# Dilated attention turned in strands of two heads and two classes, with turns issued ahead of outputs

## The chip, the core and the metric

The program runs on one core of one Trainium2 chip. TensorE (PE) multiplies, VectorE (DVE) and ScalarE (ACT) copy its results out of PSUM and do the pointwise work, GpSimd (POOL) does pointwise work on SBUF, and SyncE (SP) issues nearly all DMAs. The metric is device microseconds for one execution.

## What is computed

Attention over 4 batch entries and 8 heads of 576 positions and 64 features, all in fp32, then a mixture of 8 experts over the 2304 tokens, then a second feed-forward layer. Heads 0 to 3 look at the last 32 positions (plain), heads 4 to 7 at every fourth of the last 128 (dilated):

```python
scores = scale * np.matmul(q, k.transpose(0, 1, 3, 2))
mask_plain = (rel >= 0) & (rel < window)                                    # window = 32
mask_dil = (rel >= 0) & (rel < window * dilation) & (rel % dilation == 0)   # dilation = 4
attn = np.exp(scores - scores.max(-1)); attn = attn / attn.sum(-1)          # masked scores: -1e9
attn_out = np.matmul(attn, v)
...
out += P[:, e:e + 1] * (np.maximum(x @ w1[e], 0.0) @ w2[e])                 # 8 experts, P by 8 normalizations
out = g(out @ w_in) @ w_out
```

## The kernel before

The attention runs in eight stages n = 0 to 7: stage n is batch entry n // 2, plain heads where n is even, dilated heads where it is odd. In a dilated stage a position is 4 i + r; positions of one class r (0 to 3) only see each other, so that 576 positions fall into four runs of 144 in which the dilated window is a plain window of 32. The kernel reads queries, keys and values in that order (`classes`, L634) and treats both kinds alike afterwards.

Each stage has three blocks g of 192 positions and each block two groups h, one for each half of TensorE's rows: 48 groups in all, and a group is one step of the schedule. Work on one group:

- `load_qk` (L698) brings queries and keys into `at.big` in six pieces of 96 positions, 256 bytes in a row; one home serves stages 0 and 2 to 7, and another stage 1. `load_v` (L709) brings values.
- `turn_qk` (L726) transposes a third of the queries or keys of a stage (tile pt, four transposes of 96 columns), and VectorE copies pt to qt or kt (L740, L744). `turn_plan` (L840) says at which step which third is turned.
- `Group.both` (L757) makes the scores s of an even group and the odd one after it with 12 matmuls; in stages 0 and 1 the mask is added by TensorE, later by VectorE (L782). `scores` takes the maximum, `exps` (L786) three exponentials with their sums on ScalarE, `norm` (L793) divides on POOL.
- `Group.turn` (L799) transposes e (tile pe, three transposes) and copies it to et, by VectorE for odd groups (L806) and by ScalarE for even ones (L808).
- `Group.out` (L810) multiplies et of both groups by the values (tile px, 12 matmuls, of 64 columns each), and both engines copy px to xf (L831, L833).

`attention_steps` (L861) issues the step i as: scores of group i, norm of i - 2, query and key turns, exps of i - 1, then, at odd i, the output of i - 4, then the turn of i - 3. It yields four times a step. From the end of stage 1 on the caller weaves in the first expert's products (ph, py) and the gate (pg) at every fourth yield; `share` says how many. `first_weights` (L1017) loads that expert's weights in quarters, the first matrix of which is split into high and low parts at steps 9 to 12, and `plain_x` does the same with the first block of its input. After the attention all remaining matmuls follow, 128 x 128 products without a break.

The order on every engine is the order of the program. PSUM has eight banks; pe, px and, from stage 3 on, pt share two of them (tag "t"), and a tile waits until its bank's last tile has been copied out. SP's queue issues DMAs one after another, and each waits until the one eight before it has landed.

Of the kernel before, what the change touches and what calls it, by code (L numbers as in the profile page):

```python
# [27 lines left out]
def tile_attention_moe_ffn(ctx: ExitStack, tc, q, k, v, w_gate, w1, w2, w_in, w_out, out):  # L28
# [605 lines left out]
    def classes(d, a, n):  # L634
# [58 lines left out]
    def raw_of(n, which):  # L693
        t0 = 0 if n == 1 else 6
        return (at.big[:CH, t0 + 3 * which:t0 + 3 * which + 3, :].rearrange("p a e -> p (a e)")
                .rearrange("p (c h x) -> p c h x", c=S // CH, h=HQ))

    def load_qk(n, which, t, second=None):  # L698

        b, d = kinds[n]  # L700
        raw = raw_of(n, which)
        src = (q, k)[which][b, d * HQ:(d + 1) * HQ]
        for c in (2 * t, 2 * t + 1):
            for off, r, i, m in classes(d, c * CH, CH):
                x = (src.rearrange("h (i r) e -> r i h e", r=DILATION)[r, i:i + m] if d
                     else src[:, i:i + m].rearrange("h i e -> i h e"))
                (second if second and c % 2 else nc.sync).dma_start(out=raw[off:off + m, c], in_=x)

    def load_v(n, g, pool):  # L709
# [4 lines left out]
        else:  # L714
            t = pool.tile([KW, JG, HQ, D], F32, tag="v", bufs=4, name=f"v{n}_{g}")
        src = v[b, d * HQ:(d + 1) * HQ]
        for j in range(JG):
            for off, r, i, m in classes(d, key0(g * JG + j), KW):
                x = (src.rearrange("h (i r) e -> r i h e", r=DILATION)[r, i:i + m] if d
                     else src[:, i:i + m].rearrange("h i e -> i h e"))  # L720
                nc.sync.dma_start(out=t[off:off + m, j], in_=x)
# [4 lines left out]
    def turn_qk(n, which, t, tag):  # L726


        raw = raw_of(n, which)
        third = S // 3  # L730
        pt = bank(tag, at.bufs[tag], f"pt{n}_{which}_{t}")[:, :NPAIR * third].rearrange(
            "p (a x) -> p a x", a=NPAIR)
        for pr in range(NPAIR):
            for i in range(2):
                nc.tensor.transpose(pt[:, pr, i * CH:(i + 1) * CH],
                                    raw[:, 2 * t + i, 2 * pr:2 * pr + 2, :].rearrange("p h e -> p (h e)"),
                                    ident[:CH, :CH])
        to = (at.qt, at.kt)[which][n % 2][:, :, t * third:(t + 1) * third]
# [4 lines left out]
        else:  # L743
            nc.vector.tensor_scalar(out=to, in0=pt, scalar1=SCALE, scalar2=None, op0=ALU.mult)  # L744

    class Group:
# [52 lines left out]
        def turn(self):  # L799
# [3 lines left out]
            self.et = self.pool.tile([KW, JG, P], F32, tag="et", bufs=2, name="et")  # L803
# [6 lines left out]
        def out(self, vt):  # L810
# [9 lines left out]
            for pr in range(NPAIR):  # L820
                c = d * NPAIR + pr
                for off, r, i, m in classes(d, g * JG * QB, JG * QB):
                    while m:

                        n0 = b * S + (DILATION * i + r if d else i)
                        step = DILATION if d else 1
                        k, x = divmod(n0, PASS)
                        w = min(m, -(-(PASS - x) // step))
                        dst = xf[:, k, c, x:x + (w - 1) * step + 1:step]
                        if pr:  # L830
                            nc.vector.tensor_copy(out=dst, in_=px[:, pr, off:off + w])  # L831
                        else:
                            nc.scalar.activation(out=dst, in_=px[:, pr, off:off + w], func=AF.Copy)  # L833
# [585 lines left out]
```

## Time and profile before

| | |
|---|---|
| median of 3 runs | 1970.97 us (1967.09 to 1972.43) |
| profiled execution | 1966.19 us, span 1964.4 us |
| PE busy | 1933.1 us (98%), 13223 matmuls |
| VectorE, ScalarE, POOL busy | 1484.5, 994.5, 313.8 us |
| mean granted TensorE clock | 0.993 |
| DMA | 539.45 MB, mean 275 GB/s |
| chain that ended last | PE 92%, DVE 4%, ACT 2%, DMA 1% |

PE is the bottleneck by its busy share, but a share over the whole span mixes the attention, about a tenth of it, with the long rest. The page's 40 slices, of 49 us each, keep them apart. In rows of the order of time the number in brackets is the time an engine stood idle before the row, and behind it is what ended that. A matmul in fp32 leaves two records, a transpose one. The end of a matmul is modelled, so idle times of PE are somewhat short.

### The profile page before, as it was taken

What the parts mean: (1) busy time and instruction counts of PE and PEld (TensorE: products, weight loads), DVE (VectorE), ACT (ScalarE), POOL (GpSimd) and SP (SyncE); (2) the same over time, 40 slices, a digit from 0 to 9 for tenths busy, and PEclk for the clock granted to TensorE, in tenths of its full rate; (3) what the DMA queues carried; (4) which work ended last, traced back from release to release, by engine and by line L of the source; (5) the groups of instructions that cost most, each with busy time, mean ns of one, the idle gap of its engine ahead of it and who ended that gap; (6) DMA issues with size and microseconds to landing.
All of it is one profiled execution on the core that took longest, in us unless ns stands there. A gap on an engine that the chain in (4) does not pass through costs nothing.

```text
span 1964.4 us, 34940 instructions
## 1 busy us (share of the span) xinstructions
PE 1933.1 (98%) x13223; PEld 1839.7 (94%) x13223; DVE 1484.5 (76%) x2632; ACT 994.5 (51%) x2131; POOL 313.8 (16%) x327
## 2 busy tenths in 40 slices
PE   7899999999999999999999999999999999999999
PEld 5777889899898989999999999999999999999999
DVE  6755698888888868686888668678886576876867
ACT  4545545454555445544445435434454455675555
POOL 4213133434535400001001000010010000000000
PEclk8899999999999999999999999999999999999999
DMA  7532577788788888899889977988898877787874
GB/s 176 117 74 82 204 269 279 300 315 306 295 321 306 335 335 307 304 324 331 288 317 332 317 264 285 343 295 317 294 334 308 285 253 279 263 290 267 290 242 144
DMA packets 222392, 539.45 MB, mean 275 GB/s; under 512 B 81040, under 2 KB 113296, under 8 KB 199824
## 3 DMA queue, kind: packets, MB, share of 16 engines
q1 hardware_dynamic: 220624, 536.82, 77.6%
q8 instruction: 105, 1.72, 0.4%
q10 hardware_dynamic: 1600, 0.39, 0.1%
q14 instruction: 63, 0.52, 0.1%
HBM read 383.53 MB, written 153.62 MB: 273 GB/s over the span
## 4 chain that ended last, share of the span: by engine, by line
PE 92%; DVE 4%; ACT 2%; DMA 1%; issue 0%; SPq 0%; ACTq 0%; DVEq 0%
PE pa L414 22%; PE py L414 16%; PE pc L414 11%; PE qy L414 9%; PE qh L414 9%; PE qt L414 9%; PE pb L414 5%; PE qs L414 3%; PE ph L414 3%; PE qx L414 1%; PE px L818 1%; PE s L769 1%; PE pe L802 1%; DMA w_kept<-raw 1%; DVE et L806 1%
## 5 line engine op out<-in xcount | busy, mean ns | idle before, releaser
L414 PE MATMUL pa<-xo,w1o 128*128 128x384 f32 x2736 | 512.9, 335 | 4.0 <-ACT kept L429 2.9
L414 PEld LDWEIGHTS pa<-xo,w1o 128*128 128x128 f32 x2736 | 476.3, 188 | 8.0 <-ACT kept L429 4.5
L414 PE MATMUL pc<-xo,w1o 128*128 128x384 f32 x1368 | 257.1, 335 | 0.8 <-DVE w1o L112 0.8
L138 POOL TENSOR_TENSOR raw<-raw 128x256 f32<-128x256 f32 x152 | 140.3, 952 | 701.5 <-DVE raw L326 170.4
L414 PE MATMUL py<-w2o,hh 128*128 128x512 f32 x816 | 251.5, 389 | 0.0
L414 PEld LDWEIGHTS pc<-xo,w1o 128*128 128x128 f32 x1368 | 238.5, 188 | 1.1 <-DVE w1o L112 1.1
L429 ACT ACTIVATE kept<-pa 128x384 f32<-128x384 f32 x228 | 110.2, 491 | 233.4 <-PE pa L414 231.7
L414 PEld LDWEIGHTS py<-w2o,hh 128*128 128x128 f32 x816 | 152.8, 188 | 30.3
L387 DVE TENSOR_TENSOR xf<-xf 128x768 f32<-128x768 f32 x180 | 167.3, 964 | 1.4
L414 PE MATMUL py<-w2o,hl 128*128 128x512 f32 x408 | 158.7, 389 | 0.0
L112 DVE TENSOR_TENSOR w1o<-raw,w1o 128x256 fp32r<-128x256 f32 x210 | 130.3, 671 | 9.8 <-ACT w1o L111 9.8
L111 ACT ACTIVATE third<-xf 128x768 fp32r<-128x768 f32 (+1 forms) x124 | 95.3, 793 | 80.7 <-DVE xf L387 33.1
L112 DVE TENSOR_TENSOR third<-xf,third 128x768 fp32r<-128x768 f32 (+1 forms) x124 | 117.7, 961 | 21.2 <-ACT third L111 19.0
L414 PE MATMUL pb<-xo,w1o 128*128 128x384 f32 x684 | 128.9, 335 | 0.0
L432 DVE TENSOR_TENSOR kept<-pb,kept 128x384 f32<-128x384 f32 x114 | 62.0, 554 | 85.7 <-PE pb L414 85.0
L1162 ACT ACTIVATE xf<-kept 128x384 f32<-128x384 f32 x168 | 86.2, 523 | 69.0 <-DVE kept L432 67.3
L414 PEld LDWEIGHTS pb<-xo,w1o 128*128 128x128 f32 x684 | 119.1, 188 | 0.0
L111 ACT ACTIVATE w1o<-raw 128x256 fp32r<-128x256 f32 x210 | 77.3, 414 | 67.6 <-POOL raw L138 67.6
L111 ACT ACTIVATE hh<-xf 128x768 fp32r<-128x768 f32 x92 | 74.6, 841 | 70.5 <-DVE xf L387 33.5
L111 ACT ACTIVATE hl<-xf 128x768 fp32r<-128x768 f32 x92 | 74.5, 841 | 63.7 <-DVE xf L387 25.9
L604 ACT ACTIVATE hh<-kept 128x384 fp32r<-128x384 f32 x102 | 53.7, 526 | 81.1 <-DVE kept L432 81.0
L112 DVE TENSOR_TENSOR hh<-xf,hh 128x768 fp32r<-128x768 f32 x92 | 86.8, 957 | 10.1 <-ACT hh L111 10.0
(191 smaller groups left out, 3470.4 us busy)
## 6 DMA issues: line engine op xcount, KB each, us to landing
w1o<-w_kept SPq DMA_DIRECT2D x294, 512.0 KB, 5.7
w2o<-w_sums SPq DMA_DIRECT2D x56, 1024.0 KB, 5.4
w_kept<-w1o SPq DMA_DIRECT2D x105, 512.0 KB, 4.4
w2o<-w_kept SPq DMA_DIRECT2D x40, 1024.0 KB, 5.4
w2x<-w_kept SPq DMA_DIRECT2D x24, 1024.0 KB, 4.8
w2x<-w_sums SPq DMA_DIRECT2D x24, 1024.0 KB, 5.1
w_kept<-w2o SPq DMA_DIRECT2D x23, 1024.0 KB, 6.3
w_kept<-raw SPq DMA_DIRECT2D x36, 512.0 KB, 6.9
```

The lines of the kernel that those rows point to most:

```text
L111: nc.scalar.activation(out=hi, in_=raw, func=AF.Copy)
L112: return lambda: nc.vector.tensor_tensor(out=lo, in0=raw, in1=hi.bitcast(F32), op=ALU.subtract)
L138: nc.gpsimd.tensor_tensor(out=out[:, q], in0=in0[:, q], in1=in1[:, q], op=op)
L387: nc.vector.tensor_tensor(out=dst, in0=in0, in1=in1, op=ALU.subtract)
L414: nc.tensor.matmul(o, lhsT=a(h), rhs=b(l), start=first and n == 0, stop=last and n == 2, skip_group_check=on)
L429: nc.scalar.activation(out=dst, in_=src, func=AF.Copy)
L432: nc.vector.tensor_tensor(out=dst, in0=src, in1=dst, op=ALU.add)
L604: return [lambda: nc.scalar.activation(out=hi, in_=src, func=AF.Relu), lambda: nc.vector.scalar_tensor_tensor(out=lo, in0=src, scalar=0.0, ...
L769: nc.tensor.matmul(x.raw[pr * QB:(pr + 1) * QB, i, :], lhsT=qt[rows, pr, j * QB:(j + 1) * QB], rhs=kt[rows, pr, key0(j):key0(j) + KW], sta ...
L802: nc.tensor.transpose(pt[:, i * P:(i + 1) * P], self.e[:, i, :], ident)
L806: nc.vector.tensor_copy(out=self.et, in_=pt)
L1162: return [lambda: nc.scalar.activation(out=hid[:, half_, j, f], in_=src, func=AF.Relu)]
```

## The change

1. Strands. A dilated stage is cut into four strands of 144: strand t holds two heads (2 (t // 2) and the next) and two classes (2 (t % 2) and the next). A query turn takes two classes of one head, which lie side by side in memory, as its 128 rows. The loads of dilated queries and keys then have rows of 1 KB (four classes of one head), those of values 512 bytes. A dilated stage has 4 x 2 turns of four pieces (96, 48, 96 and 48 columns) in place of 3 x 2 turns of four pieces of 96. In an output of a dilated stage the half of TensorE's columns is now the head and the place in px the class.
2. Homes. Plain queries and keys live in `at.plain`, dilated ones in `at.dilated`; the loads of stage n + 2 are issued by the turns of stage n. All values of stages 0 and 1 are loaded at the start. `at.zero` moves into a corner of `at.big`.
3. Order. Within a step the turn of group i - 3 stands ahead of the output of group i - 4, with three buffers for et instead of two. Stage 1's turns move from steps 4, 5 and 7 to steps 3, 4, 6 and 7. The first weights are issued after step 3 at once.

```diff
-            for off, r, i, m in classes(d, c * CH, CH):
-                x = (src.rearrange("h (i r) e -> r i h e", r=DILATION)[r, i:i + m] if d
-                     else src[:, i:i + m].rearrange("h i e -> i h e"))
-                (second if second and c % 2 else nc.sync).dma_start(out=raw[off:off + m, c], in_=x)
+        if d == 0:
+            for c in range(2 * t, 2 * t + 2):
+                queue.dma_start(out=at.plain[:, which, c], in_=src[:, c * CH:(c + 1) * CH].rearrange("h i e -> i h e"))
+            return
+        for c, (i, m) in enumerate(SEGS):
+            queue.dma_start(out=at.dilated[:m, which, c].rearrange("p h r e -> p h (r e)"),
+                            in_=src[:, DILATION * i:DILATION * (i + m)].rearrange("h (i r) e -> i h (r e)", r=DILATION))
...
+            for pr in range(NPAIR):
+                for c, (i, m) in enumerate(SEGS):
+                    strand = at.dilated[:m, which, c, t // 2 * 2 + pr, t % 2 * 2:t % 2 * 2 + 2, :]
+                    nc.tensor.transpose(pt[:, pr, i:i + m], strand.rearrange("p r e -> p (r e)"), ident[:m, :m])
+            to = to[:, :, t * SEG:(t + 1) * SEG]
...
+        if n + 2 < NN and (d == 0 or t == DILATION - 1):
+            load_qk(n + 2, which, t)
...
-            self.et = self.pool.tile([KW, JG, P], F32, tag="et", bufs=2, name="et")
+            self.et = self.pool.tile([KW, JG, P], F32, tag="et", bufs=3, name="et")
...
-                        nc.tensor.matmul(px[h * D:(h + 1) * D, pr, i * QB:(i + 1) * QB], lhsT=vt[:, i, 2 * pr + h, :],
+                        half, x = (pr, h) if d else (h, pr)
+                        nc.tensor.matmul(px[half * D:(half + 1) * D, x, i * QB:(i + 1) * QB], lhsT=vt[:, i, 2 * pr + h, :],
                                          rhs=et[h][:, i, pr * QB:(pr + 1) * QB], start=True, stop=True)
...
-            for t in range(NG):
+            first = PER * n
+            for t in range(DILATION if n % 2 else NG):
...
                     elif n == 1:
-                        at_step(first - (2 if t == 0 else 3), "middle", n, w, t, "y")
+                        at_step(first + (-3, -2, 0, 1)[t], "middle", n, w, t, "y")
...
             turn(i, "late")
             yield done
+            if lo <= i - 3 < hi:
+                at.groups[i - 3].turn()
+            yield done
             if lo <= i - LAG < hi and (i - LAG) % 2:
                 x = at.groups[i - LAG]
                 x.out(at.vts[x.n, x.g])
...
-            yield done
-            if lo <= i - 3 < hi:
-                at.groups[i - 3].turn()
             yield done
...
-                if n == 4 * 5:
-                    for x in (("qk", 2, 0), ("v", 1, 0), ("v", 1, 1), ("qk", 2, 1)):
-                        load(*x)
-                        pull(first)
-                    load("v", 1, 2)
-                    load("qk", 2, 2)
+                if n == 4 * 3:
+                    pull(first, KC)
                     load_gate()
```

What the change does to the order of PE in the even part of the attention, at stage 3's first output (s: scores, pt: query or key turn, pe: turn of e, ph: expert products, px: output). Before:

```order
L802 MATMUL pe<-ident,e 96x128 x3
L769 MATMUL s<-kt_152,qt_150 64x96 x12
L735 MATMUL pt_0_1_1242<-ident,big 128x96 x4
L414 MATMUL ph_2_1208<-xo_66,w1o_73 128x384 x6
L414 MATMUL ph_3_1263<-xo_63,w1o_74 128x384 x3
L802 MATMUL pe<-ident,e 96x128 x3
L735 MATMUL pt_1_1_1280<-ident,big 128x96 x4
L818 MATMUL px<-et,v_0_981 64x64 x12
L414 MATMUL ph_3_1263<-xo_63,w1o_74 128x384 x3
L414 MATMUL ph_3_1263<-xo_66,w1o_76 128x384 x6
```

After:

```order
L782 MATMUL s<-kt_150,qt_148 64x96 x12
L739 MATMUL pt_0_1_1245<-ident,plain 128x96 x4
L815 MATMUL pe<-ident,e 96x128 x3
L414 MATMUL ph_2_1217<-xo_66,w1o_73 128x384 x6
L414 MATMUL ph_3_1272<-xo_63,w1o_74 128x384 x3
L739 MATMUL pt_1_1_1283<-ident,plain 128x96 x4
L815 MATMUL pe<-ident,e 96x128 x3
L832 MATMUL px<-et,v_0_986 64x64 x12
L414 MATMUL ph_3_1272<-xo_63,w1o_74 128x384 x3
L414 MATMUL ph_3_1272<-xo_66,w1o_76 128x384 x6
```

The turn of the odd group (first pe) has moved ahead of the step's expert products, and the turn of the even group from behind the output to right ahead of it. The same place with the semaphores that are waited for, before:

```order
L735 MATMUL pt_1_1_1280<-ident,big 128x96 [waits DMAHW6_49,DVE_49]
L735 MATMUL pt_1_1_1280<-ident,big 128x96 [waits DMAHW7_49]
L735 MATMUL pt_1_1_1280<-ident,big 128x96 x2
L818 MATMUL px<-et,v_0_981 64x64 [waits DMAHW0_49,DVE_49]
L818 MATMUL px<-et,v_0_981 64x64
L818 MATMUL px<-et,v_0_981 64x64 [waits DMAHW1_49]
```

and after, at this output and at the next one:

```order
L739 MATMUL pt_1_1_1283<-ident,plain 128x96 [waits DVE_49]
L739 MATMUL pt_1_1_1283<-ident,plain 128x96 [waits DMAHW4_49]
L739 MATMUL pt_1_1_1283<-ident,plain 128x96 x2
L815 MATMUL pe<-ident,e 96x128 [waits DVE_49,Pool_49]
L815 MATMUL pe<-ident,e 96x128 x2
L832 MATMUL px<-et,v_0_986 64x64 [waits DMAHW4_49,Activation_49]
```

```order
L739 MATMUL pt_1_2_1391<-ident,plain 128x96 [waits DVE_49]
L739 MATMUL pt_1_2_1391<-ident,plain 128x96 x3
L748 MATMUL pt_0_0_1399<-ident,dilated 128x96 [waits DMAHW0_49,DVE_49]
L748 MATMUL pt_0_0_1399<-ident,dilated 128x48 [waits DMAHW1_49]
L748 MATMUL pt_0_0_1399<-ident,dilated 128x96
L748 MATMUL pt_0_0_1399<-ident,dilated 128x48
L815 MATMUL pe<-ident,e 96x128 [waits DVE_49,Pool_49]
L815 MATMUL pe<-ident,e 96x128 x2
L832 MATMUL px<-et,v_1_1090 64x64 [waits DMAHW2_49,DVE_49]
```

The output waited for VectorE in the kernel before. Here it waits for ScalarE in the first piece (px has the bank of the pe right ahead of it, which ScalarE copies) and for VectorE in the second (px has the bank of the second pt). Of the 17 outputs from stage 2's second block on, five name ScalarE, eight VectorE for a pt of the same step, and the last four VectorE for et itself, with more work between than before.

PE in the start, behind stage 0's last turns, before:

```order
L735 MATMUL pt_0_2_315<-ident,big 128x96 x4
L735 MATMUL pt_1_2_321<-ident,big 128x96 x4
L802 MATMUL pe<-ident,e 96x128 x3
L763 LDWEIGHTS identb
L763 MATMUL s<-mask,identb 128x288
L763 LDWEIGHTS identb
L763 MATMUL s<-mask,identb 128x288
L769 MATMUL s<-kt_151,qt_149 64x96 x12
L735 MATMUL pt_0_0_364<-ident,big 128x96 x4
L735 MATMUL pt_1_0_370<-ident,big 128x96 x4
L802 MATMUL pe<-ident,e 96x128 x3
L735 MATMUL pt_0_1_425<-ident,big 128x96 x4
```

After:

```order
L739 MATMUL pt_0_2_327<-ident,plain 128x96 x4
L739 MATMUL pt_1_2_335<-ident,plain 128x96 x4
L748 MATMUL pt_0_0_354<-ident,dilated 128x96
L748 MATMUL pt_0_0_354<-ident,dilated 128x48
L748 MATMUL pt_0_0_354<-ident,dilated 128x96
L748 MATMUL pt_0_0_354<-ident,dilated 128x48
L748 MATMUL pt_1_0_360<-ident,dilated 128x96
L748 MATMUL pt_1_0_360<-ident,dilated 128x48
L748 MATMUL pt_1_0_360<-ident,dilated 128x96
L748 MATMUL pt_1_0_360<-ident,dilated 128x48
L815 MATMUL pe<-ident,e 96x128 x3
```

Stage 1's first turns (here pt_0_0 and pt_1_0 of stage 1) have moved ahead of the first turn of e and of stage 0's last score products. SP's queue at that time, with the first rows after the second block's values, before:

```order
L707 DMA big<-in_k_dram 96x4x64 x2
L721 DMA v_1_204<-in_v_dram 96x4x64 x3
L721 DMA v_2_208<-in_v_dram 96x4x64 x3
L707 DMA big<-in_q_dram 96x4x64
L707 DMA big<-in_q_dram 48x4x64 x2
L707 DMA big<-in_k_dram 96x4x64
L707 DMA big<-in_k_dram 48x4x64 x2
```

After:

```order
L702 DMA plain<-in_k_dram 96x4x64 x2
L723 DMA v_1_205<-in_v_dram 96x4x64 x3
L705 DMA dilated<-in_q_dram 96x4x256
L705 DMA dilated<-in_q_dram 48x4x256
L705 DMA dilated<-in_k_dram 96x4x256
L705 DMA dilated<-in_k_dram 48x4x256
```

Stage 1's queries and keys have moved ahead of the third block's values and are four DMAs instead of sixteen. The first weights (the rows in_moe_w_dram) on SP's queue, before:

```order
L707 DMA big<-in_k_dram 96x4x64 x2
L1016 DMA acc<-in_moe_w_dram 128x512
L721 DMA v_0_392<-in_v_dram 96x4x64 x2
L721 DMA v_0_392<-in_v_dram 48x4x64 x2
L1016 DMA acc<-in_moe_w_dram 128x512
L721 DMA acc<-in_v_dram 96x4x64
L721 DMA acc<-in_v_dram 64x4x64
L721 DMA acc<-in_v_dram 32x4x64
L721 DMA acc<-in_v_dram 96x4x64
L1016 DMA acc<-in_moe_w_dram 128x512
L707 DMA big<-in_q_dram 96x4x64 x2
L707 DMA big<-in_k_dram 96x4x64 x2
```

After:

```order
L702 DMA plain<-in_q_dram 96x4x64 x2
L702 DMA plain<-in_k_dram 96x4x64 x2
L702 DMA plain<-in_q_dram 96x4x64 x2
L702 DMA plain<-in_k_dram 96x4x64 x2
L1031 DMA acc<-in_moe_w_dram 128x512 x4
L913 DMA gate<-in_moe_w_gate_dram 128x4x8
L705 DMA dilated<-in_q_dram 96x4x256
L705 DMA dilated<-in_q_dram 48x4x256
L705 DMA dilated<-in_k_dram 96x4x256
L705 DMA dilated<-in_k_dram 48x4x256
```

The four quarters have moved together, behind the loads of stage 2's queries and keys and with no values between.

## Rows read from the trace of the kernel before

**Rows 1.** the page's 40 slices: busy tenths of PE, its clock

```profile
PE   7899999999999999999999999999999999999999
...
PEclk8899999999999999999999999999999999999999
```

**Rows 2.** two stretches: us, busy (count) by engine, PEclk, DMA share, GB/s

```profile
0.00:25.00 25.00, 19.80 (x214) 13.67 (x216) 11.25 (x35) 10.90 (x49) 8.97 (x24) 0.86 0.76 166
...
250.00:275.00 25.00, 25.00 (x127) 22.44 (x126) 22.44 (x63) 11.12 (x27) 6.70 (x8) 1.00 0.84 301
```

**Rows 3.** waits of PE, 0 to 250 us: total, times, longest

```profile
PE px L818 <- DVE et L806: 14.8, 21, 3.0
...
PE pt L735 <- DMA big<-in_q_dram: 2.8, 4, 1.6
```

**Rows 4.** waits of PE, 60 to 190 us

```profile
PE px L818 <- DVE et L806: 8.8, 17, 1.5
```

**Rows 5.** order of time, 118 us: start, us, engine, line [idle <-releaser]

```profile
118.19 0.49 PE L802 MATMUL pe<-ident,e 128*96 128x128 f32 x3
...
118.41 0.42 PEld L735 LDWEIGHTS pt<-ident,big 96*128 96x128 f32 x4
...
118.52 0.49 PE L735 MATMUL pt<-ident,big 96*128 96x96 f32 x4
...
119.32 0.78 PEld L818 LDWEIGHTS px<-et,v 96*64 96x64 f32 x24 [0.50 <-DVE et L806]
...
119.32 0.92 PE L818 MATMUL px<-et,v 96*64 96x64 f32 x24 [0.31 <-DVE et L806]
...
120.17 1.67 PE L414 MATMUL py<-xo,xo 128*128 128x512 f32 x6
```

**Rows 6.** order of time, 124 to 127 us, the chain behind a pair's scores

```profile
124.44 0.73 PE L769 MATMUL s<-kt,qt 64*64 64x96 f32 x24
...
125.00 0.36 ACT L790 ACTIVATE e<-sm,nm 128x96 f32<-128x96 f32 x1
...
125.98 0.19 ACT L790 ACTIVATION_READ_ACCUMULATOR e<-sm,nm 128x1 f32 x1
...
126.35 0.53 DVE L744 TENSOR_SCALAR qt<-pt 128x384 f32<-128x384 f32 x1
...
126.61 0.67 POOL L797 TENSOR_TENSOR e<-e,z 128x288 f32<-128x288 f32 x1 [5.36 <-DVE z L796]
```

**Rows 7.** PE's groups by shape, 60 to 190 us: busy, mean ns

```profile
L818 PE MATMUL px<-et,v 96*64 96x64 f32 x408 | 16.9, 226 | 8.8 <-DVE et L806 8.8
...
L769 PE MATMUL s<-kt,qt 64*64 64x96 f32 x352 | 11.0, 256 | 0.0
```

**Rows 8.** order of time on PE in the start

```profile
9.70 0.88 PE L735 MATMUL pt<-ident,big 96*128 96x96 f32 x8
...
13.44 0.27 PE L735 MATMUL pt<-ident,big 96*128 96x96 f32 x1 [0.57 <-DMA big<-in_q_dram]
...
34.96 1.54 PE L818 MATMUL px<-et,v 96*64 96x64 f32 x22 [2.22 <-DVE et L806]
...
55.56 1.55 PE L818 MATMUL px<-et,v 96*64 96x64 f32 x24 [3.04 <-DVE et L806]
...
59.29 1.24 PE L769 MATMUL s<-kt,qt 64*64 64x96 f32 x24
```

**Rows 9.** order of time on SP's queue in the start

```profile
7.18 3.10 SPq L721 DMA_DIRECT2D v<-in_v_dram  x6
...
30.39 0.48 SPq L1016 DMA_DIRECT2D acc<-in_moe_w_dram  x1
```

**Rows 10.** order of time on VectorE in the start

```profile
33.95 0.49 DVE L103 CAST w1o<-acc 128x256 fp32r<-128x256 f32 x2 [2.15 <-DMA acc<-in_moe_w_dram]
...
52.17 2.88 DVE L106 TENSOR_TENSOR xo<-xf,xo 128x768 fp32r<-128x768 f32 x2
```

**Rows 11.** one microsecond of the start, columns as in rows 2

```profile
4.00:5.00 1.00, 1.00 (x7) 0.84 (x6) 0.00 (x0) 0.10 (x1) 0.86 (x4) 1.00 1.29 208
```

More of the change, by code (lines that the diff above doesn't have):

```diff
@@ L632, in tile_attention_moe_ffn, with strands @@
     kinds = [(b, d) for b in range(B) for d in range(2)]
-    def classes(d, a, n):
+    def strands(d, a, n):
         if d == 0:
@@ L714, in load_v @@
         else:
-            t = pool.tile([KW, JG, HQ, D], F32, tag="v", bufs=4, name=f"v{n}_{g}")
+            t = pool.tile([KW, JG, HQ, D], F32, tag="v", bufs=5, name=f"v{n}_{g}")
         src = v[b, d * HQ:(d + 1) * HQ]
         for j in range(JG):
[L718 to L721, printed above, removed]
+            for off, r, i, m in strands(d, key0(g * JG + j), KW):
+                if d:
+                    rows = src[r // 2 * 2:r // 2 * 2 + 2].rearrange("h (i r) e -> i h r e", r=DILATION)
+                    nc.sync.dma_start(out=t[off:off + m, j].rearrange("p (h r) e -> p h (r e)", h=2),
+                                      in_=rows[i:i + m, :, r % 2 * 2:r % 2 * 2 + 2].rearrange("i h r e -> i h (r e)"))
+                else:
+                    nc.sync.dma_start(out=t[off:off + m, j], in_=src[:, i:i + m].rearrange("h i e -> i h e"))
         return t
@@ L726, in turn_qk @@
     def turn_qk(n, which, t, tag):
[L729 to L738, printed above, removed]
+        d = kinds[n][1]
+        to = (at.qt, at.kt)[which][n % 2]
+        pt = bank(tag, at.bufs[tag], f"pt{n}_{which}_{t}")
+        if d == 0:
+            third = S // 3
+            pt = pt[:, :NPAIR * third].rearrange("p (a x) -> p a x", a=NPAIR)
+            for pr in range(NPAIR):
+                for i in range(2):
+                    nc.tensor.transpose(pt[:, pr, i * CH:(i + 1) * CH],
+                                        at.plain[:, which, 2 * t + i, 2 * pr:2 * pr + 2, :].rearrange("p h e -> p (h e)"),
+                                        ident[:CH, :CH])
+            to = to[:, :, t * third:(t + 1) * third]
+        else:
+            pt = pt[:, :NPAIR * SEG].rearrange("p (a x) -> p a x", a=NPAIR)
+            for pr in range(NPAIR):
+                for c, (i, m) in enumerate(SEGS):
+                    strand = at.dilated[:m, which, c, t // 2 * 2 + pr, t % 2 * 2:t % 2 * 2 + 2, :]
+                    nc.tensor.transpose(pt[:, pr, i:i + m], strand.rearrange("p r e -> p (r e)"), ident[:m, :m])
+            to = to[:, :, t * SEG:(t + 1) * SEG]
         if which:
@@ L985, in tile_attention_moe_ffn @@
             at.kt = [pool.tile([P, NPAIR, S], F32, name=f"kt{i}") for i in range(2)]
-            at.big = pool.tile([P, 12, DM], F32, name="big")
+            at.big = pool.tile([P, 6, DM], F32, name="big")
+            at.plain = pool.tile([CH, 2, S // CH, HQ, D], F32, name="plain")
+            at.dilated = pool.tile([CH, 2, 2, HQ, DILATION, D], F32, name="dilated")
+            at.zero = at.big[:, 5, :256].bitcast(BF16)
+            nc.vector.memset(at.zero, 0.0)
             at.staged = 0
@@ L999, in tile_attention_moe_ffn @@
             at.vts = {}
-            def load(what, n, t):
-                if what == "v":
-                    at.vts[n, t] = load_v(n, t, pool)
-                else:
-                    for w in range(2):
-                        load_qk(n, w, t, nc.scalar if (n, t) in ((0, 0), (0, 1)) else None)
-            for x in (("qk", 0, 0), ("qk", 0, 1), ("v", 0, 0), ("qk", 0, 2), ("v", 0, 1), ("v", 0, 2),
-                      ("qk", 1, 0), ("qk", 1, 1), ("qk", 1, 2)):
-                load(*x)
+            for t in range(2):
+                load_qk(0, 0, t)
+                load_qk(0, 1, t, nc.scalar)
+            at.vts[0, 0] = load_v(0, 0, pool)
+            for w in range(2):
+                load_qk(0, w, 2)
+            at.vts[0, 1] = load_v(0, 1, pool)
+            for w in range(2):
+                load_qk(1, w)
+            for x in ((0, 2), (1, 0), (1, 1), (1, 2)):
+                at.vts[x] = load_v(*x, pool)
             busy(7)
```

44 lines of the change are left out of this document (17 added, 27 removed).

## The prediction

> **What bounds the kernel now.** I read the page's slices first, then the windows, then who waits for whom on PE, then the order of time on all engines around the attention, and last the groups by shape. The slices say that TensorE is busy 9 tenths or more in all but the first two, and that its clock is below full only there [rows 1]. So the change has to be paid or earned in the attention, which ends before 190 us; what follows is moved as a block, microsecond for microsecond, since PE has no idle time there (25.00 of 25 us in the window from 250 [rows 2]). In the first 25 us PE has 19.80 busy, at a clock of 0.86. PE's longest wait is an output px for VectorE's copy of et: 14.8 us in 21 times; next come query turns waiting for their load, 2.8 us [rows 3]. Of the 14.8 us, 8.8 in 17 times fall after 60 us, in the even part of the attention [rows 4]; the other 6.0 belong to the start.
>
> The reader should see the form of that wait in one pair of groups: the odd group's turn pe starts at 118.19, and the output that needs VectorE's copy of it at 119.32, 1.13 us later [rows 5]. Of these PE fills 0.33 with the three transposes of pe and about 0.33 with four of pt; 0.47 is lost (the view counts 0.31, because it models a matmul's end). For 17 outputs the true loss is 8.8 + 17 x 0.16 = 11.5 us.
>
> **Turns ahead of outputs (after 60 us).** The odd group's turn now stands ahead of its step's expert products, and its copy is long done when the output comes; but the even group's turn stands right ahead of the output. What takes the old wait's place is in the order rows with semaphores: of 17 outputs, 5 wait for ScalarE's copy of the turn just ahead of them, 8 for VectorE's copy of a query or key turn of the same step, and the last 4 for et with work between. The chain behind a pair of scores is the same in both kernels: scores end at 124.44 + 0.73 = 125.17, ScalarE's three exps run from 125.00 to 126.17 (1.17 us), VectorE is through mask add, maximum, sum and reciprocal when it begins a turn's copy at 126.35, and POOL's e is ready at 126.61 + 0.67 = 127.28 [rows 6]. From these, with expert products as long as now:
> - 3 outputs behind ScalarE's copy with ScalarE free: about 1.1 us from turn to output, 0.33 covered, 0.75 lost: 2.25.
> - 2 behind a copy that queues after a relu and three exps: 1.3 and 0.8.
> - 6 behind VectorE's copy of pt, under long expert products: 0.43 each, 2.6.
> - 2 where two turns pt stand in one step and VectorE copies both first: 1.25 each, 2.5.
> - the last 4: no wait at the output, but two turns wait for POOL's e, 0.9 together.
>
> Sum 10.3 against 11.5: **-1.2 us**. Bounds: -6 if each of the 13 costs 0.43 and the last four nothing; +5 if each of the 13 costs 1.25, as where VectorE's four score operations (1.2 us, from 125.17 to 126.35) stand ahead of the copy. Queued behind a waiting output are the expert products and the next scores, and with them every engine of the attention.
>
> **Two classes of one head in an output (12 of 24).** Today the 12 products of an output alternate between the two halves of TensorE's columns. They leave 24 records between 119.32 and 120.17, 35 ns apart [rows 5], while one lasts 226 ns at 64 columns and a score product's 256 at 96 [rows 7]: (256 - 226) / 32 = 0.94 ns a column, and a turn's 0.08 us for 96 columns (below) gives 0.83, so that 64 columns occupy their half for 53 to 60 ns. A spacing of 35 then needs both halves beside each other. In a dilated output of the new kernel 12 records in a row go to one half, then 12 to the other. One after another they take 24 x 53 = 1.28 us instead of 0.85: 0.43 more. Nine of the twelve lie after 60 us: **+3.9 us**; the three of the start hide in waits for VectorE. Lower bound 0 (the halves don't set the pace); upper bound 1.2 each, 10.9, if the weight loads, 0.78 us for 24 [rows 5], no longer hide (1.28 + 0.78 - 0.85). I take 0.43, nearest to the rows.
>
> In these rows weights and products of turns do overlap although both use the same 96 rows: loads 118.41 to 118.83, products 118.52 to 119.01, together 0.60 us where one after the other would be 0.91 [rows 5]. The Trainium skill, in "TensorE: Matmul & The Clock Gate", section "Part 3: Packing small matmuls — row/col tiling", says that a weight load overlaps with running matmuls only where the row group differs. By that rule nothing of a half's loads would hide and outputs would pay the upper bound; this trace does not agree with it for the turns, and for outputs of one half it has no row. It is a rival below, priced from the rows.
>
> **More, smaller turns.** A dilated stage turns 8 x 4 pieces (half of 96, half of 48 columns) instead of 6 x 4 of 96; the columns are the same. Four of 96 take 0.49 us with one tail: (0.49 - 0.25) / 3 = 0.08 each [rows 5, 7]. A piece of 48 costs half of that if columns set the pace and the same if not: 0 to 0.65 us a stage. I take 0.25, for three stages after 60 us: **+0.8 us** (0 to 2). VectorE copies the same columns in 8 pieces for 6, beside PE's work.
>
> **The start (to 60.53, the end of the scores begun at 59.29 [rows 8]).** Four parts.
> - *Lost, early.* PE is through with stage 0's turns at 9.70 + 0.88 = 10.58 and now meets stage 1's at once (order rows). SP issues values up to about 8.7 (half of the 3.10 us from 7.18 [rows 9]), then the four DMAs of 1 KB rows. Ahead of them are 18 DMAs of 98 KB, 1.77 MB, at 208 GB/s with a DMA share of 1.29 [rows 11]: until 10.5. The queries' 0.59 MB then takes 1.6 us (301 GB/s at a share of 0.84 [rows 2], so 358) to 2.8 (208) and about 1 us to land: 13 to 14.4, the keys 15 to 17. Today PE meets its first late load at 13.44, after stage 0's last scores; now these stand behind the load. I cost this at 3 us by the end of stage 1's scores (0 to 5).
> - *Saved, weights.* The last quarter of the first weights is issued at 30.39 and used at 33.95, after VectorE has idled 2.15; the output at 34.96 has waited 2.22 and takes 1.54 for 22 records where later 24 take 0.92, so the clock has halved [rows 5, 8 to 10]. In the new order the quarters stand 44th to 47th on SP's queue, at 0.52 us each (3.10 for 6 [rows 9]) 23 to 25, and land by 29, before step 9. Saved: 2.2 and some 1.5 of half clock.
> - *Saved, the first block's input.* VectorE spends 2.88 us from 52.17 ahead of a copy of et, and the output at 55.56 has waited 3.04, and again takes 1.55 [rows 8, 10]. In the new order that copy stands ahead of it, and the output waits for ScalarE only: 2.2 earlier, and 1.1 of half clock. Late next is VectorE's mask add, which holds the following scores.
> - *Lost, steps 9 to 12.* Two more turns for stage 1 beside the weights' splits on VectorE and POOL: 1.
>
> Together 3 - 3.7 - 3.3 + 1 = **-3.0 us** (-8 to +3).
>
> **Sum.** -1.2 + 3.9 + 0.8 - 3.0 = +0.5 us on the profiled execution's 1966.19 (span 1964.4). The median of the runs shown, 1970.97, is 4.8 higher; the same step from there gives 1971.5.
>
> **Rivals.**
> - *Faster.* The halves cost nothing and the start gives 6: -1.2 + 0.8 - 6 = -6.4, 1964.6. For it: nothing in the trace shows a half alone. Against: score records of 96 columns start closer, (0.73 - 0.256) / 23 = 0.021 us, on four quarters [rows 6, 7], so that issue is not what spaces outputs by 35.
> - *Slower, one half at a time with its weights in the open.* Place: the nine dilated outputs after 60 us; price 10.9 in place of 3.9: +7.5, 1978.5. It decides as soon as a dilated output takes over 1.8 us.
> - *The wait does not go, it grows.* ScalarE's exps and VectorE's four score operations now stand between a turn and its output. With +5 in place of -1.2: +6.7, 1977.7. Against: expert products of 15 ph or py, some 3 us, cover these chains in the middle stages.
> - *The start gives nothing* (loads land at 17): +3.5, 1974.5, within the likeliest case.
>
> **How the numbers follow.** What a measurement of this kernel can tell from no change is about 0.3%, 5.9 us: 1965.1 to 1976.9. No change, centred on 1971.5: 0.44, with its own range 1965 to 1977. Faster: 0.29, the first rival and larger gains of the start. Slower: 0.27, exposed weights 0.15 and the growing wait 0.12. For 8 in 10 I let two of the four terms fall together near their bounds: -10 to +12, 1961 to 1983.
>
> **What would show it.** From 60 to 190 us, px's wait for et down from 8.8 to under 2, with new waits of px for ScalarE's et and VectorE's qt or kt, 7 to 10 in all. A dilated output 1.2 to 1.4 us from its start to the next product, a plain one 0.85. Stage 1's first query turn at 13 to 14.5. The casts of the first weights without a wait for a DMA. Stage 3's first scores ending near 57.5 instead of 60.53. I am wrong if dilated outputs take 0.85, if px waits more than 14 us, or if a stretch after 190 us changes its length.

## The result: slower by 1.4%, outside the range

| | median, us | lowest to highest | runs | granted clock |
|---|---|---|---|---|
| before | 1969.08 | 1967.09 to 1972.43 | 4 | 0.993 |
| changed | 1997.49 | 1992.89 to 2002.99 | 4 | 0.984 to 0.990 |

The ratio is 1.0145, 95% interval 1.0124 to 1.0165: 28 us lost, where the prediction had 0.5 and a range up to 1983. The profiled execution took 2002.99 us (span 2001.2, clock 0.984).

The slices of the changed kernel, beside [rows 1], show the same busy TensorE and a lower clock at the left edge:

```profile
PE   8899999999999999999999999999999999999999
...
PEclk7699999999999999999999999999999999999999
```

The windows (columns as in [rows 2]) show for how long: TensorE is at half clock for much of the first 85 us, with PE busy 22 us in 25 where its clock is 0.53.

```profile
0.00:25.00 25.00, 17.48 (x134) 10.73 (x135) 7.78 (x23) 7.00 (x29) 7.64 (x22) 0.78 0.79 166
25.00:50.00 25.00, 23.77 (x267) 17.38 (x265) 16.11 (x50) 12.14 (x62) 9.26 (x14) 0.68 0.90 209
50.00:75.00 25.00, 22.00 (x191) 15.49 (x192) 16.38 (x46) 10.54 (x44) 10.82 (x12) 0.53 0.28 68
75.00:100.00 25.00, 22.57 (x208) 19.10 (x207) 13.54 (x39) 9.60 (x41) 4.96 (x7) 0.79 0.57 114
```

The same view of the kernel before has 0.78 and 1.00 in the last two:

```profile
50.00:75.00 25.00, 21.08 (x237) 16.79 (x237) 18.97 (x50) 12.29 (x49) 9.83 (x10) 0.78 0.56 124
75.00:100.00 25.00, 23.61 (x269) 18.88 (x269) 16.81 (x51) 15.20 (x61) 4.67 (x7) 1.00 0.44 99
```

PE's waits up to 250 us (columns as in [rows 3]) have the wait of 14.8 us gone, and nothing of its size in its place. All of PE's waits there add up to 21 us; in the kernel before they add up to 24.

```profile
PE px L832 <- ACT et L821: 5.2, 8, 0.9
PE pe L815 <- DVE kt L751: 5.1, 4, 2.1
PE pt L748 <- DMA dilated<-in_q_dram: 4.2, 2, 3.4
...
PE px L832 <- DVE et L819: 0.3, 1, 0.3
```

So the time is not lost in waits but inside PE's busy time. The page of the changed kernel says the same: PE is busy for 1969.4 us where it was busy for 1933.1, 36.3 us more, and the span has grown by 36.8.

```profile
PE 1969.4 (98%) x13255; PEld 1860.9 (93%) x13255; DVE 1475.1 (74%) x2640; ACT 993.7 (50%) x2131; POOL 319.6 (16%) x327
```

The order of time on PE, beside [rows 5], has a dilated turn of four pieces and a dilated output:

```profile
106.09 1.44 PE L832 MATMUL px<-et,v 96*64 96x64 f32 x24
107.45 2.33 PE L414 MATMUL py<-w1o,xo 128*128 128x512 f32 x9
...
119.36 0.91 PE L748 MATMUL pt<-ident,dilated 96*128 96x96 f32 x4
120.20 0.53 PE L815 MATMUL pe<-ident,e 128*96 128x128 f32 x3
```

The turn holds PE for 120.20 - 119.36 = 0.84 us, though it has fewer columns (288) than a plain turn (384), which holds it for 0.33 to 0.39 up to a turn of e. The output takes 107.45 - 106.09 = 1.36 where the one of [rows 5] takes 0.85. PE's groups by line (0 to 250 us; busy, mean ns) have the turns' sum: 34.0 us for the 32 dilated ones, and 13.4 for the 24 plain ones. In the kernel before, all 48 turns took 28.2 (third fence), so the turns hold 19 of the 36 us. The outputs' groups hold another 6.6 (32.9 for 26.3). In the rows by shape (second fence) the pieces of 96 and of 48 stand apart; records of the two overlap in time, so these rows add up to more than 34.0.

```profile
L748 PE MATMUL pt<-ident,dilated 96*128 96x96 f32 (+1 forms) x128 | 34.0, 318 | 5.8 <-DMA dilated<-in_q_dram 4.2 <-DMA dilated<-in_k_dram 1.6
...
L739 PE MATMUL pt<-ident,plain 96*128 96x96 f32 x96 | 13.4, 273 | 0.0
```

```profile
L748 PE MATMUL pt<-ident,dilated 96*128 96x96 f32 x64 | 22.0, 343 | 4.3 <-DMA dilated<-in_q_dram 3.4 <-DMA dilated<-in_k_dram 0.9
...
L748 PE MATMUL pt<-ident,dilated 48*128 48x48 f32 x64 | 18.8, 294 | 1.6 <-DMA dilated<-in_q_dram 0.8 <-DMA dilated<-in_k_dram 0.8
```

```profile
L735 PE MATMUL pt<-ident,big 96*128 96x96 f32 x192 | 28.2, 276 | 4.6 <-DMA big<-in_q_dram 2.8 <-DVE qt L744 1.4 <-DVE z L796 0.2
```

Two marks place the loss: the first gate product (pg), which closes the start, and the first matmul of the routing after the attention (pm).

| profiled execution | pg, us | pm, us | span, us |
|---|---|---|---|
| before | 57.0 | 216.9 | 1964.4 |
| changed | 70.3 | 251.0 | 2001.2 |

Of the 36.8 us of the two spans, 13.3 are lost in the start, 20.8 between the marks and 2.7 behind them.

### The profile page after: what moved, and what is told of

Read it like the earlier page. It is cut to its first block, busy times and chain, and to the rows that moved or that the text cites. A ratio compares the mean times of both kernels' runs of the same rounds, so it can differ in the third digit from the quotient of the medians.

```text
span 2001.2 us, 34888 instructions
## 1 busy us (share of the span) xinstructions
PE 1969.4 (98%) x13255; PEld 1860.9 (93%) x13255; DVE 1475.1 (74%) x2640; ACT 993.7 (50%) x2131; POOL 319.6 (16%) x327
## 4 chain that ended last, share of the span: by engine, by line
PE 91%; DVE 4%; DMA 2%; ACT 2%; issue 1%; SPq 0%; POOL 0%; ACTq 0%; POOLq 0%; DVEq 0%
PE pa L414 21%; PE py L414 16%; PE pc L414 11%; PE qy L414 9%; PE qt L414 8%; PE qh L414 8%; PE pb L414 5%; PE ph L414 3%; PE qs L414 3%; DMA w_kept<-raw 2%; PE px L832 2%; PE qx L414 1%; PE pt L748 1%; PE pe L815 1%; PE s L782 1%
## 5 line engine op out<-in xcount | busy, mean ns | idle before, releaser
L112 DVE TENSOR_TENSOR w1o<-raw,w1o 128x256 fp32r<-128x256 f32 x210 | 117.9, 608 | 16.9 <-ACT w1o L111 16.9
L112 DVE TENSOR_TENSOR third<-xf,third 128x768 fp32r<-128x768 f32 (+1 forms) x124 | 113.6, 928 | 20.5 <-ACT third L111 18.3
L1173 ACT ACTIVATE xf<-kept 128x384 f32<-128x384 f32 x168 | 86.4, 525 | 70.3 <-DVE kept L432 68.6
L111 ACT ACTIVATE hl<-xf 128x768 fp32r<-128x768 f32 x92 | 74.5, 842 | 62.7 <-DVE xf L387 25.6
L112 DVE TENSOR_TENSOR hl<-xf,hl 128x768 fp32r<-128x768 f32 x92 | 87.5, 965 | 8.5 <-ACT hl L111 8.4
```

The lines of the kernel that those rows point to most:

```text
L111: nc.scalar.activation(out=hi, in_=raw, func=AF.Copy)
L112: return lambda: nc.vector.tensor_tensor(out=lo, in0=raw, in1=hi.bitcast(F32), op=ALU.subtract)
L1173: return [lambda: nc.scalar.activation(out=hid[:, half_, j, f], in_=src, func=AF.Relu)]
```

## The experiments

Theory: TensorE pays at each change between two forms of matmul. In the built programs a transpose of 96, 80 or 72 rows has the form 128 x 128 (rows by columns of TensorE), and one of 64 or 48 rows the form 64 x 128; the profile does not show the form. A dilated turn goes 96, 48, 96, 48 and a turn of e with the form 128 x 128 follows, so the form changes four times. Rivals: the small piece is dear by itself; the halves of the outputs; the late loads of stage 1 and the half clock behind them. Ratios are to the kernel before on the same chip, with 95% intervals; 0.001 is 2 us.

**1. Even pieces.**

```
-    SEGS = ((0, CH), (CH, SEG - CH))
+    SEGS = ((0, SEG // 2), (SEG // 2, SEG // 2))
```

> The changed kernel with each strand of 144 rows cut into 72 and 72 rows instead of 96 and 48, for the loads and the turns. Theory: the turn of a dilated strand is dear (0.84 us at full clock from its start to the next matmul, 0.33 to 0.39 for a turn of four equal pieces) because a piece of 48 rows stands between pieces of 96, and TensorE loses some 0.12 us at each change from one form to the other; 32 such turns are 15 us at full clock. Here no piece has 64 rows or fewer: a turn takes 0.35 to 0.45 us and the time falls from 1997.5 to 1978-1984 us, more if the half-clock stretch between 14 and 85 us also shortens (down to 1974). Rival 1, the price is of a small piece as such (four pieces of fewer columns each, eight turns more): a turn stays at 0.7 to 0.85 us and the time within 3 us of 1997.5. Rival 2, the late loads of stage 1's queries and keys and the long half clock behind them make the loss: the turn may change but the half clock stays, and at most 4 us are gained.

1985.81 us, ratio 1.0095 (1.0082 to 1.0108): 10 to 12 us back, 1.8 us short of the expectation. A turn behind score products now holds PE for 0.30 us (order of time), and the 32 take 16.9 in place of 34.0 (groups by line):

```profile
115.97 0.47 PE L748 MATMUL pt<-ident,dilated 72*128 72x72 f32 x4
116.27 0.49 PE L815 MATMUL pe<-ident,e 128*96 128x128 f32 x3
```

```profile
L748 PE MATMUL pt<-ident,dilated 72*128 72x72 f32 x128 | 16.9, 264 | 8.0 <-DMA dilated<-in_q_dram 4.7 <-DMA dilated<-in_k_dram 2.5 <-DVE kt L751 0.7
```

The turns are 17 us shorter, and the whole of PE's busy time in the two profiled executions is 25.6 us shorter (1943.8 for 1969.4). Their spans differ by 15.9 only, for PE's waits up to 250 us rise from 21 to 32 us (pe for POOL's e 0.6 to 5.2, pe for VectorE's kt 5.1 to 7.2, px for et 0.3 to 2.2): with PE faster, it waits for the other engines more often. The medians are 11.7 apart, since the profiled execution of the changed kernel was its slowest.

**2. The same pieces, like beside like.**

```
-            for pr in range(NPAIR):
-                for c, (i, m) in enumerate(SEGS):
+            for c, (i, m) in enumerate(SEGS):
+                for pr in range(NPAIR):
```

> The changed kernel with the pieces of a dilated turn in the order 96, 96, 48, 48 instead of 96, 48, 96, 48, the same pieces and the same loads. Theory (a price at each change of form): two changes in a turn instead of four, its start to the next matmul falls from 0.84 to about 0.60 us at full clock and the time by 7 to 9 us, to about 1989. Rival 1 (the small piece itself is dear): turn 0.84 and 1997.5 us, unchanged within 3 us. Rival 2 (the start and the half clock): unchanged within 3 us.

1992.84 us, 1.0128 (1.0112 to 1.0145): 3 to 5 us back where 7 to 9 were expected. The time alone would leave it open, the interval meets the changed kernel's; the trace doesn't: a turn behind score products takes 0.57 us.

```profile
111.10 0.64 PE L748 MATMUL pt<-ident,dilated 96*128 96x96 f32 x4
111.67 0.53 PE L815 MATMUL pe<-ident,e 128*96 128x128 f32 x3
...
114.76 0.58 PE L748 MATMUL pt<-ident,dilated 96*128 96x96 f32 x4
115.28 0.53 PE L815 MATMUL pe<-ident,e 128*96 128x128 f32 x3
```

What stands ahead of a turn counts too: behind expert products, as in the second pair of rows, a turn is some 0.05 us shorter than behind score products. Behind score products four changes take 0.84, two 0.57 and none 0.30; behind expert products they take 0.79 (113.66 to 114.45 in the changed kernel), 0.52 and 0.25 (119.22 to 119.47 in experiment 1). Both series give 0.13 to 0.14 us a change at full clock.

**3. Form against size.** `SEGS = ((0, 80), (80, SEG - 80))`: nearly even, but the second piece has 64 rows and so the smaller form.

> The changed kernel with strands cut into 80 and 64 rows. Sizes nearly those of 72 and 72 (1985.8 us, a turn 0.28 us to the next matmul), but the second piece is at the size at which the program gives a matmul the smaller form of 64 rows. Theory, that the price is one of each change between the two forms (0.13 us each, four in a turn): the turn is again 0.8 us and the time 1993-1999 us, that of the changed kernel. Rival, that unequal or very small pieces cost (48 rows against 96): the turn is 0.3-0.45 us and the time 1984-1988.

1999.91 us, 1.0154 (1.0138 to 1.0170), no different from the changed kernel's time, and its turn of 0.85 us. Eight rows moved from one piece to the other make the difference to experiment 1. A price of the smaller form as such is out too, for experiment 2 has as many pieces in that form and pays half. The size of the pieces is not the cause, the change of form is.

```profile
117.46 0.91 PE L748 MATMUL pt<-ident,dilated 80*128 80x80 f32 x4
118.31 0.53 PE L815 MATMUL pe<-ident,e 128*96 128x128 f32 x3
```

**4. Halves of the output alternate.**

```
-            for pr in range(NPAIR):
-                for i in range(JG):
-                    for h in range(2):
+            for y in range(2):
+                for i in range(JG):
+                    for z in range(2):
+                        pr, h = (z, y) if d else (y, z)
```

> The changed kernel with the twelve matmuls of a dilated output in an order in which the two halves of the output's partitions alternate (the pair is the innermost loop in dilated stages, the head the outermost), the same matmuls; plain stages as they are. Theory on the outputs: twelve records of 1.43 us at full clock and 2.46 at half clock fall to 0.85-0.95 and 1.55, 12 outputs are 6 to 8 us, so about 1990 us. Rival, the outputs' length comes from the moving operand or from the weights and not from the halves: 1.43 us stays and the time too, within 3 us.

1995.09 us, 1.0136 (1.0123 to 1.0149), no difference that the times resolve where 6 to 8 us were expected; but the output is back at 0.85 us, so the halves do set its pace:

```profile
97.19 0.92 PE L833 MATMUL px<-et,v 96*64 96x64 f32 x24
98.04 2.37 PE L414 MATMUL py<-w1o,xo 128*128 128x512 f32 x9
```

**5. Both edits (1 and 4).**

> Both edits together: strands cut into 72 and 72 rows, and the halves of a dilated output alternating. Theory: the two gains add, 13-20 us and 6-8 us, 1970 to 1978 us; if the clock in the first 100 us comes back to that of the kernel before, 1965 to 1972, level with it (1969). Rival 2 (the late loads at the start and the half clock behind them make the loss): 1988 or more.

1981.36 us, 1.0077 (1.0063 to 1.0091). 3 us above the expectation: the clock did not come back in most runs (0.985 to 0.993). The outputs gave some 4 us on top of experiment 1, whose interval still touches this one.

**6. On top of 5, stage 1's turns a step later:** `(-3, -2, 0, 1)` becomes `(-2, -1, 1, 2)`.

> The kernel with strands of 72 and 72 rows and alternating halves (1981.4 us), with stage 1's turns one step later: steps 4, 5, 7 and 8 instead of 3, 4, 6 and 7. In it TensorE stands 7.3 us in stage 1's turns for the dilated queries and keys, which land at 13 to 17 us. Theory that the start's late loads are the larger part of what is still lost (12 us against the kernel before): these waits fall under 3 us, the first gate product comes at 54-57 us instead of 58.8, and the time falls by 3 to 6 us, to 1975-1978. Rival: the loads come in the same order and what waited in the turns then waits in stage 1's scores or in stage 0's outputs for their input; the time stays within 2 us of 1981.4.

1980.68 us, 1.0060 (1.0047 to 1.0073), not resolved from 5, as the rival had it. The turns' wait for loads only fell from 7.3 to 5.5.

**7. On top of 5, output ahead of turn:** the block with `turn()` goes back behind the one with `out()`.

> The kernel with strands of 72 and 72 rows and alternating halves (1981.4 us), with the output ahead of the turn of e again, as in the kernel before. Prediction's term for the order: turns ahead of outputs are worth 1.2 us after 60 us (bounds 6 gained and 5 lost), so 1980 to 1985 us, with the output waiting for VectorE's copy of et again (14 us in 21 places up to 250 us, where there are now 1.3 us). Rival: the new order costs more than it saves (pe waits for VectorE's copy of the keys' turn 7.2 us, px for ScalarE's copy of et 5.7 us): 1974 to 1978 us.

1977.34 us, 1.0041 (1.0026 to 1.0056): 4 to 7 us faster, in the rival's range. The output's wait is back (14.8 us in 19 places) and yet the kernel is faster; the wait of pe for the keys' copy (7.2 us) is gone, since the output stands between the second turn and pe.

**8. The order alone, in the kernel before** (turn ahead of output, et with three buffers).

> The kernel before with one part of the change alone: the turn of e ahead of the output, and a third buffer for et. Prediction's term: 1 us gained (bounds 6 gained and 5 lost), 1964 to 1968 us beside 1967.2; the output's wait for VectorE's et (14 us up to 250 us) falls under 4 us. Rival: the wait only moves to the turn, which now waits for the e of the group or for VectorE's copies: lost 2 to 5 us. If the order were the change's gain without the rest's losses, the time falls by 4 us or more.

1967.38 us, 0.9999 (0.9989 to 1.0008): nothing that the times resolve. px's wait for VectorE's et went from 14.8 to 0.7 us, and new waits took its place:

```profile
PE px L818 <- ACT et L808: 6.6, 8, 1.4
PE px L818 <- DVE kt L740: 4.9, 8, 1.8
PE pe L802 <- POOL e L797: 4.5, 6, 1.7
```

**9. On top of 5, the turn that shares a step ahead of its scores.**

```
-                        at_step(first - 5 + 2 * t + w, "middle", n, w, t, "t")
+                        at_step(first - 5 + 2 * t + w, "before" if 2 * t + w in (0, 7) else "middle", n, w, t, "t")
```

> The kernel with strands of 72 and 72 rows and alternating halves (1981.4 us), with the dilated turn that shares a step with a plain one (two steps in twelve) put ahead of that step's scores. Theory: the turn of e waits 7.2 us in four places for VectorE's copy of the keys' turn, because two turns and the turn of e rotate through two banks; here that wait falls under 2 us and the time by 3 to 5 us, to 1976-1978. Rival: these waits are covered (what is behind them waits for ScalarE and VectorE anyway), and other waits grow: within 2 us of 1981.4.

1973.73 us, 1.0029 (1.0015 to 1.0043): 8 to 9 us faster than 5, where 3 to 5 were expected, and more than the wait itself. PE's wait of pe for the keys' copy, of 5 and of this kernel:

```profile
PE pe L815 <- DVE kt L751: 7.2, 4, 2.7
```

```profile
PE pe L815 <- DVE kt L751: 1.6, 1, 1.6
```

**10 and 11. On top of 9, stage 1's loads ahead of a v; then its turns a step later too.**

```
-            at.vts[0, 1] = load_v(0, 1, pool)
             for w in range(2):
                 load_qk(1, w)
+            at.vts[0, 1] = load_v(0, 1, pool)
```

> The kernel with even strands, alternating halves and the turns that shared a step ahead of its scores (1973.7 us), with the loads of stage 1's queries and keys issued ahead of the v of stage 0's second group instead of behind it. Theory, that the late loads of stage 1 are what is left of the loss (TensorE waits 7.7 us for them at 10 to 19 us): the waits fall to 4-5 us, the first gate product comes 2 us earlier and the time falls by 1.5 to 3 us, to 1971-1972. Rival: the v that now comes later holds the outputs of stage 0 by as much, or what is left is the eight turns more (32 dilated ones for 24): within 1.5 us of 1973.7.

> The same with stage 1's turns one step later as well (steps 4, 5, 7, 8). Theory of the late loads: the wait for them falls under 2 us, 1969 to 1971 us, level with the kernel before. Rival: within 1.5 us of 1973.7, as the later turns alone did nothing (1980.7 for 1981.4).

1973.15 and 1975.59 us, both 1.0028 (to 1.0040): nothing that the times resolve. In 10 the wait for the dilated loads fell to 4.2 us, and PE met another, for the first weights, through VectorE's cast (4.85 us) and POOL's e:

```profile
38.25 0.88 PE L815 MATMUL pe<-ident,e 128*96 128x128 f32 x3 [4.58 <-POOL e L810]
```

```profile
35.79 0.49 DVE L103 CAST w1o<-acc 128x256 fp32r<-128x256 f32 x2 [4.85 <-DMA acc<-in_moe_w_dram]
```

**12. Experiment 10 with the output ahead of the turn.**

> The kernel with even strands, alternating halves, spread turns and the earlier loads of stage 1, with the output ahead of the turn of e again. If the old order gained 4 us in the earlier pair only because it kept the turn of e from waiting behind the keys' copy, it gains nothing here: 1971 to 1976 us, equal to the kernel with the earlier loads within 2 us. Rival, that the new order costs by itself: 1968 to 1970 us.

1972.85 us, 1.0019 (1.0007 to 1.0030): equal to 10. Once no two turns stand ahead of pe, the order is worth nothing that the times resolve, as in the kernel before.

**13 to 15. What is left at the start:** on top of 10 the casts a step later (`PER + 4`, `PER + 8`); on top of 10 the weights' load at `n == 4` instead of `4 * 3`; on top of 12 the casts a step later.

> The kernel with even strands, alternating halves, spread turns and earlier stage-1 loads (1973.2 us), with the casts of the first expert's first weights one step later. In it VectorE's cast waits 4.85 us for these weights at 31 to 36 us, POOL's normalisation of e stands behind it and TensorE waits 4.6 us. Theory: this wait is what is left of the loss at the start; the first gate product comes 2 to 4 us earlier (56 to 57.5 us) and the time falls by 2 to 4 us, to 1969-1971, level with the kernel before or better. Rival: the cast's wait in the profile hides another (the half clock or stage 1's v), and the time stays within 1.5 us of 1973.2.

> The same kernel (1973.2 us), with the loads of the first weights issued two steps earlier, ahead of stage 2's last queries and keys and of stage 3's. Theory: the weights land 2 us earlier, half of the cast's wait goes, 1971 to 1972.5 us. Rival: within 1.5 us of 1973.2, since the queue is full until 30 us and the order in it changes little.

> The casts one step later in the kernel with the output ahead of the turn of e (1972.9 us). There no wait for the weights shows, but VectorE's copies of et have the output wait 13.7 us in 18 places. Theory: the casts' place does not matter here, within 1.5 us of 1972.9; the outputs' wait of 3.3 us ahead of the first gate product stays. Rival: the casts stand in front of et's copies on VectorE at 36 to 46 us, and one step later they gain 2 to 4 us.

1973.93, 1972.88 and 1972.14 us, ratios 1.0027, 1.0029 and 1.0021 (intervals within 1.0011 to 1.0040): none differs from 10. The wait of 4.6 us went in 13 and fell to 1.7 in 14, and the first gate product came at 58.6 and 57.2 us instead of 59.5: the profile moved and the time did not. So 13 and 14 came out as their rivals had it, and 15 as its theory.

No version of the changed kernel beats the kernel before. The best (12 and 15) are 0.2% behind it, the changed kernel 1.4%.

## Why the prediction was wrong

**More, smaller turns (+0.8, bounds 0 to 2): the step that failed.** It priced a piece by its columns and had no row with pieces of two forms side by side. Measured: 17 us of PE's busy time in the turns, 10 to 12 us of the run. The cause, a price at each change of form, is shown by experiments 1 to 3. The Trainium skill names a mechanism, in "TensorEngine Tiling (Array Packing)", section "Tiling Modes": changing the tiling mode, not just the tile, drains the TensorE. No trace here shows the drain itself; the 0.13 to 0.14 us a change agree with it.

**Two turns in one step (2.5, in the order's sum): found, mis-sized and put in the wrong place.** The prediction had outputs wait 1.25 us twice. In fact the turn of e waits behind the second copy, in four places, 5.1 us in the changed kernel and 7.2 with the faster turns:

```profile
141.57 0.92 PE L748 MATMUL pt<-ident,dilated 96*128 96x96 f32 x4
142.41 0.55 PE L739 MATMUL pt<-ident,plain 96*128 96x96 f32 x4
145.03 0.51 PE L815 MATMUL pe<-ident,e 128*96 128x128 f32 x3 [2.07 <-DVE kt L751]
```

Late behind pe are et, the output and the expert products. Taking the pair apart gave 8 to 9 us, of which the wait itself is 5.6. About 3 more go with the clock, whose mean over the runs rose from 0.988 (experiment 5) to 0.991 (experiment 9), at the 1 us for 0.001 worked out below; that is an estimate.

**Turns ahead of outputs (-1.2): right in size** where no two turns share a step: 0 measured, in the kernel before (8) and between 10 and 12. With the shared steps of the change the new order cost 4 to 7 us (7), around its upper bound of +5. The old wait did go, and px's new waits (5.2 us between 60 and 220) were under the 7 to 10 foreseen.

**Two classes of one head in an output (+3.9): right in the row, not resolved in time.** 1.36 us foreseen as 1.28; the time moved by 2 us (4) and by some 4 us (1 to 5), and both times the intervals touch. The price with weights in the open did not come, nor did the rival in which the output's wait grows. The rule of the Trainium skill on row groups that the prediction weighed ("TensorE: Matmul & The Clock Gate", section "Part 3: Packing small matmuls — row/col tiling") would, at the prediction's prices, have made it 1.28 + 0.78 = 2.06; this trace disagrees with it here too.

**The start (-3.0): wrong in sign.** Its first part held: the first dilated turn came at 14.16 and its keys at 17.16, just behind the 15 to 17 foreseen. Its second did not: SP issued the quarters of the first weights from 29.98 on, not at 23 to 25. The casts had no wait for a DMA, as foreseen, but the first of them came at 41.7 us, where it had come at 29.0 before; where the start is faster (10), a cast does wait 4.85 us. Stage 3's first scores ended at 71.75 + 1.24 = 72.99, not 57.5.

```profile
14.16 0.39 PE L748 MATMUL pt<-ident,dilated 96*128 96x96 f32 x1 [3.40 <-DMA dilated<-in_q_dram]
...
17.16 0.39 PE L748 MATMUL pt<-ident,dilated 96*128 96x96 f32 x1 [0.85 <-DMA dilated<-in_k_dram]
...
71.75 1.24 PE L782 MATMUL s<-kt,qt 64*64 64x96 f32 x24
...
72.92 1.31 PE L748 MATMUL pt<-ident,dilated 96*128 96x96 f32 x4
...
74.16 0.88 PE L815 MATMUL pe<-ident,e 128*96 128x128 f32 x3
```

```profile
29.98 1.89 SPq L1031 DMA_DIRECT2D acc<-in_moe_w_dram  x4
```

```profile
41.70 0.83 DVE L103 CAST w1o<-acc 128x256 fp32r<-128x256 f32 x2
```

The turns make much of it, for at half clock each holds PE for 74.16 - 72.92 = 1.24 us. With even pieces the first gate product came at 63.4, with both edits at 58.8 (in an execution at a clock of 0.993).

**Behind 190 us** the text said the rest is moved as a block: from the routing on it grew by 2.7 us of 36.8. That is no more than single executions differ by: over the seventeen profiled executions this stretch lasted 1747.4 to 1753.7 us (1747.5 before, 1750.2 changed, 1751.3 in experiment 8).

**The account, by ratios on 1968 us:** even pieces 10, halves 3 to 4, the shared steps 9, left over 4 to 6, of the 28 in all. These are steps one after another, each measured on the last, not shares that would hold in another order.

**What stays open.** The rest of 4 to 6 us. Some of it is clock: over 82 runs of the kernel before, those at a granted clock of 0.990 took 1972.3 us in the mean and those at 0.995 took 1966.8, about 1 us for 0.001. The 74 runs of experiments 9 to 15 had a mean clock of 0.9911 and 1973.9 us, those 82 had 0.9935 and 1968.4: 2.4 of the 5.5 go with the clock, and about 3 remain at equal clock. PE's busy time is no longer where they are: in the two profiles of later versions at the clock of the kernel before (0.993), those of experiments 5 and 15, PE is busy for 1932.6 and 1934.1 us against 1933.1. Their spans are longer by 8.4 and 8.2 us, nearly all of it idle time of PE, and in 15 only 2.0 of the 8.2 lie ahead of the routing. What holds the clock low in the start for longer than before wasn't found. In the changed kernel it was at half from the turn at 14.16 on, which had waited 3.40 us, and scores at 37.39 still took 1.17 us to the next row where those at 42.46 took 0.65, though PE shows no wait between 18.4 and 44. The loads, the turns' place and the casts were each tried and moved the profile without moving the time.

## What to carry to other kernels

Before cutting an operand into pieces, look at which form each piece gets (here 72 rows had one form and 64 the other): an even cut that kept all pieces in one form was worth 10 to 12 us. If the forms must mix, put like beside like. When comparing short stretches, compare those with the same work ahead of them. A wait that vanishes is worth what stands behind it on its engine: here the wait of 14.8 us was worth nothing that the times resolve, and taking 5.6 us off one behind two copies came with 8 to 9 us.

## What the runs showed of the hardware

- In these fp32 turns a change between the forms 128 x 128 and 64 x 128 costs TensorE 0.13 to 0.14 us at full clock and 0.18 at half, where a turn with four changes holds it for 1.24 us, one with two, in experiment 2, for 0.89 (60.67 to 61.56) and one of even pieces, in experiment 9, for 0.54 (56.29 to 56.83). It counts as PE's busy time and shows neither as a wait nor as one long record: the records' means, over both clocks, are 343 and 294 ns where even pieces have 264.
- Not every change of form has this price: the score products have the form 64 x 64 in the built program, and an even turn behind them holds TensorE 0.05 us longer than one behind expert products (0.30 and 0.25).
- The 24 records of an output's twelve products of 64 columns start 57 ns apart where twelve in a row go to one half of TensorE's columns (1.36 / 24), and 35 where the halves alternate (0.85 / 24).
